# Two groups of squares ordered behind a later routing step in a fused attention and mixture-of-experts kernel

## Chip, core and metric

The kernel runs on one core of one Trainium2 chip. The metric is device microseconds of one execution; the time of the kernel before is the median of three runs, 1178.45 us (1178.34 to 1178.51).

## What is computed

Attention over channels, then a mixture of experts on its output. B = 4 batches, N = 5056 tokens, C = 256 channels, 8 experts, hidden width 1024.

```python
qn = q / (norm(q, axis=1) + 1e-06);  kn = k / (norm(k, axis=1) + 1e-06)
s = kn.transpose(0, 2, 1) @ qn / tau          # 256 x 256 for each batch
a = softmax(s, axis=-1)                        # with + 1e-09 on the sum
x = (v @ a).reshape(B * N, C)                  # 20224 tokens
logits = x @ w_gate + modality_bias[modality_id]
e = argmax(logits, axis=1); gate = softmax(logits)[e]
for each expert: out[mask] = gate * (relu(x[mask] @ w1[e]) @ w2[e])
```

The norms run over the tokens, so before the softmax of a batch the kernel needs two sums over all its tokens: the products k'q (256 x 256) and the sums of the squares of q and of k.

## The kernel before, in words

**Steps.** A batch is cut into 10 steps of 512 tokens (the last has 448); step g = 10 b + s is step s of batch b. For each step two kinds of work exist. `kq_pieces(b, s)` loads q and k, adds k'q to the bank `g` in TensorE (L368), squares q and k on ScalarE (L347, four instructions) and adds the squares to `acc` on VectorE (L349, four instructions). `va_pieces(b, s)` reads v, turns it, multiplies it with the attention weights (`xp`, L588), copies the rows (`x`), adds the logits (`L`, L601) and routes the tokens: `route` chooses the expert, `place` numbers the rows (`rp` on TensorE, L646 and L647, then `pi` on VectorE, L660), and `send` scatters the rows into a table in memory, `xs`, sorted by expert (four DMA issues of GpSimd for each step, L477).

**Turning v.** Steps 0 to 5 turn v on TensorE (`vtp`, L570). From step 6 on a DMA transpose of the SP queue brings it as `T` (L537), four DMAs gather its halves as `pl` (L514), and a copy on ScalarE (L521, the high halves, which the last two of the four bring) and one on VectorE (L522) join them as `vt`.

**Blocks.** A slot is one block of 512 rows of one expert. `pick` (L700 to L730) chooses the expert on VectorE once a step has been routed, and writes `pki`; the SP queue reads it and asks for the weights (`w1r` L791, `w2r` L795) and the rows (`Tx`, a DMA transpose of `xs`, L769). Slot 0 is picked after step 2 (START = 2), slot 1 after step 3. `tr_x` joins `Tx` to `xt` (L521, L522), and ScalarE and VectorE split it into `xh` and `xl` (L833, L834). Then come the matmuls `hp` (L848) and `y` (L869). From the first block on, TensorE has block after block, with routing and k'q of later steps between.

**Order.** The program is written piece by piece with `_interleave`, and a scheduler of the framework, with durations of its own, sets from that the order of the instructions on each engine. Each engine then runs its list strictly in that order and waits on semaphores. `order(ins, others)` (L463) binds an instruction behind others of its own engine in that list; it adds no wait. `routed[g]` holds the instructions which end the routing of step g: on VectorE `pi` and a reciprocal, on ScalarE the copy of the token numbers (L662), and later the choice of the slot (L728).

**Squares deferred.** For batch 1 the squares of some steps are not written where q and k are multiplied. `split` appends them to a list (`later`, L330), the list stands in `squares` under a number, and the end of loop round g runs the list of g + 1 (L1073). When it does, `act` and `dve` (L280 to L284) bind each square and each sum behind what `behind()` returns. The lists of batch 1's steps 1 and 2 are those that the change touches; those of steps 3 and later come from `product` (L980).

**Buffers that matter.** q and k of batch 1's steps 0, 1, 4, 5 share two buffers in turn: step 5's load must wait until the squares of step 1 have been read. q and k of steps 2 and 3 stand in buffers of `w1r` and `w2r`. The squares have three buffers for q and three for k. `xp` has three PSUM banks; a bank is free when ScalarE has copied the rows and VectorE has taken the logits.

Of the kernel before, what the change touches and what calls it, by code (L numbers as in the profile page):

```python
# [20 lines left out]
def _interleave(*streams):  # L21

    lists = [list(s) for s in streams if len(s) > 0]
    total = [len(x) for x in lists]
    at = [0] * len(lists)
    while any(a < n for a, n in zip(at, total)):
        i = min(
            (i for i in range(len(lists)) if at[i] < total[i]),
            key=lambda i: ((at[i] + 0.5) / total[i], i),
        )  # L30
        lists[i][at[i]]()
        at[i] += 1
# [3 lines left out]
def kernel(  # L36
# [40 lines left out]
    START = 2  # L77
# [103 lines left out]
    def pad_rows():  # L181

        ins = nc.sync.dma_start(
            xs[E * CAP : E * CAP + BLK, :].rearrange("(p t) c -> p t c", t=BLK // P),
            pad[0].bitcast(I32).unsqueeze(1).to_broadcast([P, BLK // P, XW]),
        )
        pads.append(ins.ins)
        tc.declare_no_dep(
            ins.ins, group="xr", reason="no expert has rows there"
        )  # L190
# [66 lines left out]
    def setup_bias(b, behind=()):  # L257
        shape = [P, NS * TT, E]
        bs = bsel[b] = p2.tile(shape, F32, tag="bsel", name=f"bsel_{b}")
        tmp = p1.tile(shape, F32, tag="btmp", name=f"btmp_{b}")  # L260
        for t, is_it, i in ((bs, ALU.is_ge, 1), (tmp, ALU.is_lt, 0)):
            ins = nc.vector.scalar_tensor_tensor(
                t, m1[:, b].rearrange("p s t -> p (s t)").unsqueeze(2).to_broadcast(shape), 0.5,
                small["mb"][:, i : i + 1, :].to_broadcast(shape), is_it, ALU.mult,
            )
            order(ins.ins, [i for n, i in behind if n == "dve"])
        nc.vector.tensor_tensor(bs, bs, tmp, ALU.add)
# [206 lines left out]
    routed = {}  # L474
# [20 lines left out]
    def slots_by(g):  # L495

        return max(0, g + 1 - START - sum(x <= g for x in SKIP))

    def lag(g):

        n = LAG
        for x in SKIP:
            n -= g >= x + n
        return n
# [424 lines left out]
    def run(pieces):  # L929
        for f in pieces:  # L930
            f()
# [19 lines left out]
    def once(blk, what):  # L951
        key = (blk["slot"], what)
        if key not in done:
            done.add(key)
            run(blk[what])

    def block_stream(blk, nxt):

        once(blk, "load")
        once(blk, "prep")  # L960
        body = list(blk["body"])
        if nxt is not None:
            once(nxt, "load")
            done.add((nxt["slot"], "prep"))
            split0, turn, split1 = nxt["prep"]
            for o, f in reversed(list(zip((7, 10, 13), (split0, lambda: turn(blk["evicted"][NJ - 3]), split1)))):
                body.insert(o, f)
        before = open_blk[0]["last"] if open_blk[0] is not None else []
        for i, f in enumerate(open_blk[0]["stores"] if before else []):
            blk["beside"].setdefault(2 + i, []).append(f)  # L970
        open_blk[0] = blk
        if not before:
            return [blk["first"]] + body
        return [blk["first"], before[0], body[0]] + before[1:] + body[1:]
# [17 lines left out]
    def ask(n):  # L992
        if n < len(tasks) and n not in loaded:
            loaded.add(n)
            product(n)[0]()

    def products_of(g):

        out = []
        for n, (at, b, i) in enumerate(tasks):  # L1000
            if at == g:
                out += [lambda n=n: ask(n)] if g <= first_block else []
                out += product(n)[1:]
                if g >= first_block and (b, i) != (1, NS - 1):
                    out.append(lambda n=n: ask(n + (1 if g == first_block else 2)))
        if g == first_block + 1:
            out.append(lambda: ask(min(n for n in range(len(tasks)) if tasks[n][0] > g) + 1))
        return out
# [1 line left out]
    va = [va_pieces(*divmod(g, NS)) for g in range(G)]  # L1010
    va[0][2]()
    run(va[0][0])
    squares = {1: [], 2: []}
    for s in BEFORE:
        if s == 0:
            run(kq_pieces(1, s))
        else:
            run(kq_pieces(1, s, lambda: routed[0], squares[s]))
    pad_rows()
    for g in range(G):  # L1020
        b, s = divmod(g, NS)
        streams = []
        for gg, blk in waiting:
            if gg <= g + 1 - lag(g + 1):
                once(blk, "load")
        if len(waiting) > 0 and waiting[0][0] <= g - lag(g):
            _, blk = waiting.pop(0)
            streams.append(block_stream(blk, waiting[0][1] if waiting and waiting[0][0] <= g + 1 - lag(g + 1) else None))
        soft = list(softmax_pieces(b)) if s == 0 and b > 0 else []
        begun = []  # L1030
        if g + 1 == first_block:
            split0, turned, split1 = waiting[0][1]["prep"]
            done.add((0, "prep"))
            begun = [split0, split1]
        own = list(va[g][1])
        if g - 1 in HELD:
            t = HELD[g - 1]
            own.insert(t + 1, lambda: va[g - 1][4]([copied[g, t]]))
        turn = []
        if g + 1 < first_block:  # L1040
            turn.append(va[g + 1][2])
        turn += va[g + 1][0] if g + 1 < G else []
        if g + 1 == first_block:
            turn.append(va[g + 2][2])
        if g == first_block:
            turn.append(va[g + 2][2])
        if first_block <= g + 2 < G:
            turn.append(va[g + 2][3])
        if g + 3 == first_block or first_block + 2 < g + 3 < G:
            turn.append(va[g + 3][2])  # L1050
        if g < first_block:
            streams.append(soft + turn + begun + own)
        else:
            streams.append(soft + own[:2] + turn[:1] + own[2:5] + turn[1:] + own[5:])
        if b + 1 < B:
            if b == 0 and s == 1:
                streams.append(list(kq_pieces(1, 2, lambda: routed[1], squares[2])))
            else:
                streams.append(products_of(g))
        _interleave(*streams)  # L1060
        if waiting and waiting[0][0] <= g + 1 - lag(g + 1):
            blk = waiting[0][1]
            once(blk, "load")
            if blk["slot"] == 0:
                turned(blk["evicted"][-1])
            once(blk, "prep")
        if s == NS // 2 + 2 and b < B - 1:
            setup_bias(b + 1, routed[g])
        n = slots_by(g)
        while chosen < n:  # L1070
            waiting.append((g, block_pieces(g, chosen, pick(g, chosen, False), False)))
            chosen += 1
        run(squares.get(g + 1, []))  # L1073
        if g == NS - 1:
            ask(min(n for n in range(len(tasks)) if tasks[n][0] > g) + 1)
# [84 lines left out]
```

## Time and profile before

| what | value |
|---|---|
| median of the runs | 1178.45 us |
| profiled execution, its own time | 1175.55 us |
| span from first to last instruction in it | 1173.7 us |
| PE busy | 1153.6 us (98%) |
| VectorE busy | 920.8 us (78%) |
| ScalarE busy | 806.1 us (69%) |
| GpSimd busy | 384.7 us (33%) |
| first matmul of a block (`hp`, slot 0) | 98.62 us |
| PE idle from 93.04 to 98.62 us, as one stretch before `hp` | 5.58 us |
| PE idle for k'q between 154 and 162 us | 1.8 us |

Times inside the program count from the first instruction of the span. PE is TensorE, DVE is VectorE, ACT is ScalarE, POOL is GpSimd, SP is the queue from which nearly all DMAs are issued; a row of an issuing queue has a q behind the engine. Names carry no buffer numbers in the profile, so the step or slot of a row follows from its place in the order. A k'q product of an unsplit step is one matmul in the program and two in the profile, since its operands are full float32.

### The profile page before, as it was taken

The numbers are of one execution on the slowest core, as the hardware profiler recorded it, in microseconds if no ns is written. First come the engines' busy times: TensorE is split into PE (matmuls) and PEld (weight loads), VectorE is DVE, ScalarE is ACT, GpSimd is POOL, SyncE is SP. The second block draws the span as 40 slices with busy tenths as digits, with TensorE's granted clock in tenths as the row PEclk, the third lists the DMA queues.
The fourth block names the chain that finished last, engine by engine and source line by source line (L and its number), as shares of the span: only waits on it lengthen the run. The fifth ranks groups of instructions, "written<-read, shape, count | busy, mean of one in ns | idle before, by whom it ended". The sixth has DMA issues, their size and how long they took to land.

```text
span 1173.7 us, 23358 instructions
## 1 busy us (share of the span) xinstructions
PE 1153.6 (98%) x7708; PEld 1054.6 (90%) x7708; DVE 920.8 (78%) x2591; ACT 806.1 (69%) x1655; POOL 384.7 (33%) x345
## 2 busy tenths in 40 slices
PE   8998999999999999999999999999999999999997
PEld 7896989999999999999999999999999999999997
DVE  6787989898888888888888888878777776686552
ACT  6676867877777777687777677767656666556553
POOL 0053333323333332333333333333333333344122
PEclk9998999999999999999999999999999999999999
DMA  8979999688777677759777776765876665464421
GB/s 293 307 236 230 269 239 255 173 248 217 199 200 201 196 192 206 208 159 234 204 209 203 210 202 162 167 182 158 207 218 172 187 176 158 134 178 136 136 86 35
DMA packets 285843, 228.38 MB, mean 195 GB/s; under 512 B 185064, under 2 KB 243944, under 8 KB 285712
## 3 DMA queue, kind: packets, MB, share of 16 engines
q1 hardware_dynamic: 270032, 185.19, 60.3%
q0 software_dynamic: 15680, 41.61, 10.4%
q8 instruction: 62, 1.02, 0.4%
q14 instruction: 69, 0.57, 0.2%
HBM read 128.79 MB, written 43.43 MB: 147 GB/s over the span
## 4 chain that ended last, share of the span: by engine, by line
PE 84%; issue 6%; DMA 5%; POOL 2%; DVE 2%; ACT 1%; SPq 0%; POOLq 0%; DVEq 0%; ACTq 0%
PE y L869 34%; PE hp L848 33%; PE xp L588 9%; PE g L368 6%; DMA k<-in_k_dram 2%; POOL out_dram L477 2%; DMA q<-in_q_dram 1%; DMA Tx<-xs 1%; DMA xs<-x,pi 0%; DMA pl<-T 0%; PE vtp L570 0%; PE gw L437 0%; ACT xt L521 0%; SPq L305 0%; PE atp L431 0%
## 5 line engine op out<-in xcount | busy, mean ns | idle before, releaser
L869 PE MATMUL y<-w2h,hh 128*128 128x256 f32 x1256 | 354.5, 282 | 0.0
L869 PE MATMUL y<-w2l,hh 128*128 128x256 f32 x1256 | 351.2, 280 | 0.0
L869 PE MATMUL y<-w2h,hl 128*128 128x256 f32 x1256 | 349.4, 278 | 0.1
L477 POOL DMA_INDIRECT xs<-x,pi x160 | 196.7, 1229 | 364.0 <-DVE pr L711 183.4
L477 POOL DMA_INDIRECT out_dram<-yo,gt x158 | 174.2, 1103 | 392.1 <-ACT hh L851 297.6
L848 PE MATMUL hp<-xh,w1h 128*128 128x512 f32 (+1 forms) x640 | 250.7, 392 | 5.6 <-ACT xh L833 5.6
L848 PE MATMUL hp<-xl,w1h 128*128 128x512 f32 (+1 forms) x640 | 250.7, 392 | 0.0
L848 PE MATMUL hp<-xh,w1l 128*128 128x512 f32 (+1 forms) x640 | 249.5, 390 | 0.0
L852 DVE SCALAR_TENSOR_TENSOR hl<-hp,hh 128x512 fp32r<-128x512 f32 (+1 forms) x320 | 216.7, 677 | 36.3 <-ACT hh L851 34.6
L869 PEld LDWEIGHTS y<-w2h,hh 128*128 128x128 f32 x1256 | 236.4, 188 | 9.3
L869 PEld LDWEIGHTS y<-w2l,hh 128*128 128x128 f32 x1256 | 236.4, 188 | 8.5
L851 ACT ACTIVATE hh<-hp 128x512 fp32r<-128x512 f32 (+1 forms) x320 | 188.7, 590 | 69.2 <-PE hp L848 69.0
L869 PEld LDWEIGHTS y<-w2h,hl 128*128 128x128 f32 x1256 | 235.3, 187 | 0.4 <-DVE hl L852 0.3
L814 ACT CAST w1h<-w1r 128x512 fp32r<-128x512 f32 x160 | 99.4, 621 | 166.4 <-PE hp L848 165.6
L821 DVE TENSOR_TENSOR w1l<-w1r,w1h 128x512 fp32r<-128x512 f32 x160 | 109.8, 686 | 91.1 <-ACT w1h L814 90.4
L848 PEld LDWEIGHTS hp<-xh,w1l 128*128 128x128 f32 x640 | 120.6, 188 | 26.0
L848 PEld LDWEIGHTS hp<-xh,w1h 128*128 128x128 f32 x640 | 120.4, 188 | 19.5 <-ACT xh L833 5.8
L848 PEld LDWEIGHTS hp<-xl,w1h 128*128 128x128 f32 x640 | 120.8, 189 | 13.4
L821 DVE TENSOR_TENSOR w2l<-w2r,w2h 128x512 fp32r<-128x512 f32 x160 | 109.8, 686 | 12.6 <-ACT w2h L814 11.3
L814 ACT CAST w2h<-w2r 128x512 fp32r<-128x512 f32 x160 | 100.8, 630 | 21.7 <-PE y L869 20.1
L588 PE MATMUL xp<-ah,vh 128*128 128x264 f32 x320 | 92.7, 291 | 0.1
L600 DVE COPY x<-xp 128x256 uint16<-128x256 uint16 x136 | 56.9, 419 | 45.5 <-ACT x L599 45.1
(161 smaller groups left out, 1817.1 us busy)
## 6 DMA issues: line engine op xcount, KB each, us to landing
w1r<-in_moe_w_dram SPq DMA_DIRECT2D x80, 512.0 KB, 4.7
w2r<-in_moe_w_dram SPq DMA_DIRECT2D x80, 512.0 KB, 4.6
q<-in_q_dram SPq DMA_DIRECT2D x35, 512.0 KB, 9.4
k<-in_k_dram SPq DMA_DIRECT2D x35, 512.0 KB, 5.5
pl<-T SPq DMA_DIRECT2D x120, 128.0 KB, 4.6
v<-in_v_dram SPq DMA_DIRECT2D x6, 512.0 KB
xs<-x,pi POOLq DMA_INDIRECT x160, 4.8
out_dram<-yo,gt POOLq DMA_INDIRECT x158, 3.2
```

Source lines behind the costliest of these rows:

```text
L368: nc.tensor.matmul(gram[b][:, m, :], x, y, start=first and m == 0 and i == 0, stop=last and i == len(seq) - 1, skip_group_check=True,)
L477: ins = nc.gpsimd.indirect_dma_start(out=dst, out_offset=bass.IndirectOffsetOnAxis(ap=idx, axis=0), in_=rows, in_offset=None, bounds_check ...
L588: nc.tensor.matmul(xp[:, 0:DE], a[:, h, t * P : (t + 1) * P], w[:, h, :], start=i == 0, stop=i == len(seq) - 1,)
L600: copied[g, t] = nc.vector.tensor_copy(planes[:, 0, :], halfwords[:, 0, :]).ins
L814: ins = nc.scalar.copy(hi, src).ins
L821: evicted[-1] = [ins, nc.vector.tensor_tensor(lo, src, hi.bitcast(F32), ALU.subtract).ins]
L848: nc.tensor.matmul(hp[:, 0:rows], w[:, h, fs], x[:, h, 0:rows], start=i == 0, stop=i == len(seq) - 1)
L851: relu = nc.scalar.activation(hh[:, 0:rows], hp[:, 0:rows], AF.Relu).ins
L852: low = nc.vector.scalar_tensor_tensor(hl[:, 0:rows], hp[:, 0:rows], 0.0, hh[:, 0:rows].bitcast(F32), ALU.max, ALU.subtract).ins
L869: ins = nc.tensor.matmul(y, a[:, tsl], w[:, j % 2, :], start=(j == 0 and i == 0 and t % per == 0), stop=(j == NJ - 1 and i == 2), skip_gro ...
```

## The change

The squares and sums of batch 1's steps 1 and 2 were run at the end of loop rounds 0 and 1, behind the routing of steps 0 and 1. Both lists now stand under the number 3, are run at the end of round 2, and are bound behind the routing of step 2 and the choice of slot 0. Nothing is added or left out: the same 8 squares on ScalarE and 8 sums on VectorE run, on the same data.

```diff
-    squares = {1: [], 2: []}
+    squares = {START + 1: []}
     for s in BEFORE:
         if s == 0:
             run(kq_pieces(1, s))
         else:
-            run(kq_pieces(1, s, lambda: routed[0], squares[s]))
+            run(kq_pieces(1, s, lambda: routed[START], squares[START + 1]))
...
             if b == 0 and s == 1:
-                streams.append(list(kq_pieces(1, 2, lambda: routed[1], squares[2])))
+                streams.append(list(kq_pieces(1, 2, lambda: routed[START], squares[START + 1])))
             else:
                 streams.append(products_of(g))
```

The scheduler then orders all engines anew between step 0 and about slot 4. Three places matter here. In the rows the first number behind a name is the step (for `xp`, `L`, `rp`, `pi`, `vt`, `pl`, `T`), the batch and step (for `q`, `k`, `sq`), or the slot (for `Tx`, `xt`, `xh`, `hp`, `w1r`); the last number only counts tiles.

TensorE, what stands around the row-number matmuls `rp` of step 2. Before:

```order
L588 MATMUL xp_3_3_915<-ah_0_440,vh_3_749 128x264
L588 MATMUL xp_3_3_915<-al_0_441,vh_3_749 128x264
L646 LDWEIGHTS trim_93
L646 MATMUL rp_2_819<-chosen_of_98,trim_93 128x40
L588 MATMUL xp_3_3_915<-ah_0_440,vl_3_750 128x264
L647 LDWEIGHTS onesb_86
L647 MATMUL rp_2_819<-run_2_814,onesb_86 128x40
```

Now:

```order
L588 MATMUL xp_3_0_884<-ah_0_440,vl_3_726 128x264
L368 MATMUL g_1_487<-q_1_3_860,k_1_3_862 128x256 x2
L646 LDWEIGHTS trim_93
L646 MATMUL rp_2_795<-chosen_of_98,trim_93 128x40
L368 MATMUL g_1_487<-q_1_3_860,k_1_3_862 128x256
L647 LDWEIGHTS onesb_86
L647 MATMUL rp_2_795<-run_2_790,onesb_86 128x40
```

Before, all eight k'q products of batch 1's step 3 and nearly all `xp` of step 3 stood ahead of `rp` of step 2; now two of the products and the first of the four `xp` do.

VectorE, behind the choice of slot 0 (`pki_0`), now:

```order
L726 CAST pki_0_830<-pk_0_828 1x2
L349 TENSOR_TENSOR acc_1_488<-acc_1_488,sq_1_1_0_q_834 128x2x256
L730 TENSOR_TENSOR nxt9_121<-nxt9_121,pr_0_820 128x9
L349 TENSOR_TENSOR acc_1_488<-acc_1_488,sq_1_1_0_k_837 128x2x256
L349 TENSOR_TENSOR acc_1_488<-acc_1_488,sq_1_1_1_q_840 128x2x256
L349 TENSOR_TENSOR acc_1_488<-acc_1_488,sq_1_1_1_k_843 128x2x256
L349 TENSOR_TENSOR acc_1_488<-acc_1_488,sq_1_2_0_q_846 128x2x256
L349 TENSOR_TENSOR acc_1_488<-acc_1_488,sq_1_2_0_k_849 128x2x256
L349 TENSOR_TENSOR acc_1_488<-acc_1_488,sq_1_2_1_q_852 128x2x256
L349 TENSOR_TENSOR acc_1_488<-acc_1_488,sq_1_2_1_k_855 128x2x256
L575 TENSOR_TENSOR vl_4_865<-vtp_4_1_875,vh_4_864 128x512
L601 TENSOR_TENSOR L_3_728<-xp_3_0_884,bsel_0_458 128x8
```

Before, four of these sums stood behind `pi` of step 0 and four behind `pi` of step 1; now all eight stand in one block ahead of the second half of step 4's v and of step 3's logits.

ScalarE, where the rows of slot 0 are turned (- before, + now):

```order
 L521 COPY xt_0_0_1270<-Tx_0_1133 128x512
 L521 COPY xt_0_1_1275<-Tx_0_1133 128x512
+L521 COPY vt_7_0_1394<-pl_7_1157 128x512
 L595 COPY x_5_991<-xp_5_3_1206 128x512
+L662 COPY x_5_991<-tokid_100 128x4
 L833 CAST xh_0_1268<-xt_0_0_1270 128x512
-L662 COPY x_5_991<-tokid_100 128x4
 L833 CAST xh_0_1268<-xt_0_1_1275 128x512
```

The first copy of step 7's v, `vt_7_0`, stood behind the third `hh` of slot 0 before; now it stands ahead of `xh` of slot 0. On the SP queue the order is the same up to the first use of `T_8`: `Tx_0`, the second weights of slot 0, the transpose `T_7`, the first `w1r` of slot 1, and the four `pl_7`. Behind `T_8` the row loads `Tx_2` and `Tx_3` now stand ahead of, instead of behind, the loads of q and k of step 6 and of the weights of slot 2.

## Prediction

> **What bounds the kernel now.** I read the page's busy times first, then the waits of PE in the first 250 us, then windows, chain and rows around the first block.
>
> ```profile
> PE 1153.6 (98%) x7708; PEld 1054.6 (90%) x7708; DVE 920.8 (78%) x2591; ACT 806.1 (69%) x1655; POOL 384.7 (33%) x345
> ```
>
> ```profile
> PE hp L848 <- ACT xh L833: 5.6, 1, 5.6
> PE g L368 <- DVE qs L324: 1.6, 2, 1.1
> ...
> PE g L368 <- DVE ks L324: 0.2, 1, 0.2
> ```
>
> PE is busy in 98% of the span. The columns of the waits are total us, times, longest: behind the start-up, PE stands still for 5.6 us once, ahead of the first block, and for 1.8 us (1.6 + 0.2) in k'q between 155 and 161 us. Every other delay is hidden behind PE's own work. So a change between these places moves the end only if it moves the first `hp`, closes the 1.8 us, or makes a new stop.
>
> The chain of waits (start, length) and the last rows ahead of `hp`:
>
> ```profile
> 82.39 5.62 DMA xs<-x,pi
> ...
> 88.72 7.49 DMA Tx<-xs
> 96.23 0.50 ACT xt L521
> ...
> 98.05 0.53 ACT xh L833
> ```
>
> ```profile
> 98.62 1.22 PE L848 MATMUL hp<-xh,w1h 128*128 128x512 f32 x2 [5.58 <-ACT xh L833]
> ```
>
> The first block starts when step 2's last scatter has landed (88.01), `Tx_0` has been asked for (88.72) and landed (96.21), and ScalarE has made `xt` and `xh`. PE stops from 93.04 (98.62 - 5.58) to 98.62. The stop also costs clock; in the windows (edges, length, busy time and instructions of PE, PEld, DVE, ACT, POOL, then PE's granted clock):
>
> ```profile
> 94.00:96.00 2.00, 0.00 (x0) 0.00 (x0) 0.00 (x0) 0.00 (x0) 0.00 (x0) 1.00 1.06 309
> 96.00:98.00 2.00, 0.00 (x0) 0.00 (x0) 0.91 (x4) 1.77 (x4) 0.00 (x0) 0.77 1.78 285
> 98.00:99.00 1.00, 0.38 (x1) 0.38 (x2) 0.79 (x4) 1.00 (x4) 0.68 (x1) 0.50 0.08 23
> ...
> 103.00:104.00 1.00, 1.00 (x5) 0.48 (x3) 0.00 (x0) 0.90 (x2) 0.60 (x1) 0.55 1.05 401
> 104.00:105.00 1.00, 1.00 (x7) 0.80 (x8) 0.60 (x6) 0.47 (x2) 0.00 (x0) 1.00 1.01 359
> ```
>
> A mean of 0.77 in 96 to 98 puts the fall to 0.50 at 97.1, 4.0 us into the stop; 0.55 in 103 to 104 puts the return at 103.9. PE thus works at half clock for 5.3 us (98.6 to 103.9), a loss of 2.65 us beside the 5.58.
>
> **The change, part by part.**
>
> *Sums and squares leave routing 0 and 1.* They are 8 of each:
>
> ```profile
> 60.98 0.68 DVE L349 TENSOR_TENSOR acc<-acc,sq_q 128x512 f32<-128x512 f32 x1
> 61.58 0.68 DVE L349 TENSOR_TENSOR acc<-acc,sq_k 128x512 f32<-128x512 f32 x1
> ```
>
> One sum starts 0.60 us behind the other: 8 x 0.60 = 4.8 us of VectorE, of which PE saw nothing. The squares run on ScalarE, which is less loaded; moving them costs nothing while ScalarE is ahead of VectorE there, and 8 squares at some 0.6 us would be another 4.8 us if it were not.
>
> *Step 2's row numbers come earlier.* On TensorE six of eight k'q products and 17 of 24 `xp` no longer stand ahead of `rp`.
>
> ```profile
> 68.66 3.62 PE L368 MATMUL g<-q,k 128*128 128x256 f32 x16
> ...
> 74.14 0.28 PE L588 MATMUL xp<-ah,vh 128*128 128x264 f32 x1
> 74.26 0.28 PE L588 MATMUL xp<-al,vh 128*128 128x264 f32 x1
> ```
>
> Eight products (16 in the profile) took 3.62 us, six take 2.7; `xp` start 0.12 apart, 17 take 2.1. Together 4.8 us earlier for `rp` and `pi` of step 2.
>
> ```profile
> 73.98 0.98 POOL L477 DMA_INDIRECT xs<-x,pi  x1 [0.30 <-issue]
> 78.54 0.98 POOL L477 DMA_INDIRECT xs<-x,pi  x1 [3.58 <-ACT x L662]
> ```
>
> GpSimd stood idle for 3.58 us ahead of step 2's scatter (78.54); its last issue of step 1 (73.98) moves earlier as well, since step 1 is spared its own four sums. So the 4.8 us pass through the four issues and the landing, and `Tx_0` is asked for at 83.9 instead of 88.72. Its rows land at 83.9 + 7.5 = 91.4. Were that all, `xh` would be ready 2.4 us later, at 93.8, and the stop would be nearly closed.
>
> *`vt_7_0` stands in the way.* The order of ScalarE now has `vt_7_0`, `x_5`, and the token copy ahead of `xh` of slot 0. An engine runs its list in order, so the first block now waits for `pl_7`, which the SP queue asks for behind `Tx_0`, the weights and `T_7`:
>
> ```profile
> 88.72 2.43 SPq L769 DMA_TRANSPOSE Tx<-xs  x1
> ...
> 93.08 5.84 SPq L537 DMA_TRANSPOSE T<-in_v_dram  x1
> 99.81 0.39 SPq L791 DMA_DIRECT2D w1r<-in_moe_w_dram  x1
> 101.05 2.65 SPq L514 DMA_DIRECT2D pl<-T  x4
> ```
>
> ```profile
> DMA to landing us min/median/max: 4.5/5.1/5.8
> ```
>
> Before, `T_7` was asked for 4.4 us behind `Tx_0`, the first `pl_7` 12.3 behind it, and the last of the four (0.68 apart, 2.65 in all) 14.4 behind it. This piece of SP's list is unchanged and moves as a whole, so the last `pl_7` is asked for at 83.9 + 14.4 = 98.3 and lands, by the median of the second view, at 103.4. `pki_1`, which stands in that list, is no obstacle: VectorE made the choice of slot 1 near 83 and will be some 5 us later, near 88, while SP comes to it at about 94. What ScalarE then still has to do:
>
> ```profile
> 97.48 0.57 ACT L595 COPY x<-xp 128x512 uint16<-128x512 uint16 x1
> 97.94 0.62 ACT L833 CAST xh<-xt 128x512 fp32r<-128x512 f32 x1
> 98.46 0.20 ACT L662 COPY x<-tokid 128x4 int32<-128x4 int32 x1
> 98.56 0.62 ACT L833 CAST xh<-xt 128x512 fp32r<-128x512 f32 x1
> ...
> 108.07 0.76 ACT L521 COPY vt<-pl 128x512 uint16<-128x512 uint16 x1
> 108.70 0.62 ACT L347 ACTIVATE sq_q<-q 128x512 f32<-128x512 f32 x1
> ```
>
> By the distances of their starts `vt` takes 0.63, `x` 0.46, the token copy 0.10, and from `xh` to `hp` it was 98.62 - 97.94 = 0.68. So `hp` starts at 103.4 + 1.9 = 105.3 instead of 98.62: **+6.7 us**. With the landing at 4.5 or 5.8 it is +6.1 or +7.4.
>
> *Where the 4.8 us of sums go.* They stand as a block on VectorE ahead of step 4's `vl` and step 3's logits. The routing of step 4 ended on VectorE at 91.4 and will at about 96:
>
> ```profile
> 91.37 0.16 DVE L705 TENSOR_TENSOR pr<-end,nxt 128x9 f32<-128x9 f32 x1
> ```
>
> `rp` of step 4 and some 18 `xp` behind it (2.2 us) stand ahead of `hp` on PE, so PE comes to `hp` at 97 to 98.5. The stop that begins there covers the block; without that stop it would cost 4 to 5 us against the 93.04 at which PE now comes. The same work stands ahead of `hp` on PE before and now, so nothing else changes sides.
>
> *The clock.* The new stop is 7 to 8 us long, longer than the 4.0 after which the clock fell. `hp` again starts at half clock and pays the same 2.65: net 0. Bounds: 0 to +0.5, if a cold clock lasts a little longer this time.
>
> *The 1.8 us at 155 to 161.* There VectorE waited for step 9's `pl`.
>
> ```profile
> 128.00 1.41 ACT L521 COPY vt<-pl 128x512 uint16<-128x512 uint16 x2 [2.13 <-DMA pl<-T]
> ...
> 149.19 0.78 ACT L521 COPY vt<-pl 128x512 uint16<-128x512 uint16 x1 [2.76 <-DMA pl<-T]
> ```
>
> ScalarE was held 2.76 us by it. PE's work shifts by 6.7 us, while SP's list does so only by part: `Tx_0` to `pl_7` are 4.8 us earlier, and `Tx_2`, `Tx_3` now stand ahead of the q and k loads. `pl_9` should thus come 2 us or more earlier against PE and close the gap. I take -1.8; bounds 0 and -1.8, since no more can be won where PE has no other gap.
>
> **Sum:** +6.7 + 0 - 1.8 = +4.9 us. The profiled execution would go from 1175.55 to 1180.5; the run median, 2.9 above that execution, to 1178.45 + 4.9 = **1183.4 us**.
>
> **The rivals.**
>
> *A: a shorter way to `pl_7`.* For step 6 the same two DMAs stood closer:
>
> ```profile
> 55.12 3.18 SPq L537 DMA_TRANSPOSE T<-in_v_dram  x1
> ...
> 60.73 1.30 SPq L514 DMA_DIRECT2D pl<-T  x2
> ```
>
> That is 5.6 us from `T` to `pl`, where step 7 took 8.0 beside the still running `Tx_0`. With 5.6, and a landing of 4.7, `hp` starts 2.8 us sooner, at 102.5: +3.9 - 1.8 = +2.1, 1180.5. Against it: `T_7` still follows `Tx_0` at the same distance. The stop would be 4.0 to 5.5 us, so the clock might just stay up (-2.65 more), but mostly not.
>
> The row for that is the fall 4.0 us into the stop, at 97.1. [...]
>
> *B: faster.* Were `pl_7` there by the time PE comes to `hp`, the first block would start at about 97.8, without the half clock: -0.8 - 2.65 - 1.8 = -5.2, 1173.2. That needs `pl_7` landed by 97.8 - 1.9 = 95.9, 12.0 us behind `Tx_0`'s start. The shortest rows give 4.4 + 5.6 + 2.0 (first to last `pl`) + 4.5 = 16.5. It decides itself at that one place, and no row comes near it.
>
> *C: longer.* `x_5` is held behind `vt_7_0` too, so step 5's routing and its scatter are late by 6 to 7 us. `Tx_2` waits for the scatter of step 4, whose token copy stands behind `x_5`, and it now stands ahead of the q and k loads of step 6 and of slot 2's weights. Then `pl_9` is no earlier, the 1.8 us stay, and about 2 us join them at 120 to 160 us: +6.7 + 2 = +8.7, 1187.2. For it:
>
> ```profile
> 105.79 3.13 SPq L769 DMA_TRANSPOSE Tx<-xs  x1
> ...
> 117.09 0.52 SPq L305 DMA_DIRECT2D q<-in_q_dram  x1
> 121.46 2.58 SPq L514 DMA_DIRECT2D pl<-T  x4
> ```
>
> SP is the queue on which all this hangs, and a held `Tx_2` holds the loads behind it. Against it: between 105.79 and 117.09 there are 11 us with few issues, and a block of PE's work lies ahead of each.
>
> *D: the change doesn't do what it says.* If ScalarE's squares or the token copy hold step 2's scatter where it was, `Tx_0` stays at 88.72 and `pl_7` lands at 108.2: `hp` at 110.1, +11.5 - 1.8 = +9.7, 1188.2. In the order the squares stand behind the routing, so this is unlikely.
>
> **How the numbers follow.** Main 0.64, A 0.13, B 0.05, C 0.15, D 0.03. The main case's own range is 1181.4 to 1186.0: a landing of 4.5 to 5.8 us (-0.6 to +0.7), SP's piece up to 1 us shorter because step 2's rows meet less traffic, and 0 to 1.8 us of recovery. The 8-in-10 range adds A below and most of C above: 1180.0 to 1187.0. A measurement of this kernel tells 0.2% (2.4 us) from no change, so "same" is 1176.1 to 1180.8. It holds two thirds of A and a sliver of the main case, 0.11; faster is B and A without the half clock, 0.06; slower is the rest, 0.83.
>
> **What would show it.** The scatter of step 2 should start near 73.7 and `Tx_0` near 83.9; if not, D. ScalarE should idle for some 10 us ahead of one `vt`, released by the DMA `pl`, and then run `vt`, `x`, token copy, `xh` in a row, with `hp` at 104.5 to 106; a `hp` near 102.5 is A. PE's longest wait should be 7 to 8 us, with the clock at 0.50 for about 5 us behind it. The k'q waits near 160 should be gone; if they stay or grow, C. The forecast is wrong if `hp` starts at or before 98.6, or if PE has a new stop of over 1 us after 106.

## The result

The changed kernel took 1187.20 us (median of 6 runs, 1185.72 to 1188.44) beside 1178.48 us for the kernel before in the same series (a series is a set of runs of both kernels made side by side): a ratio of 1.0079, with a 95% interval of 1.0064 to 1.0093. It is slower, as forecast, by 8.7 us where 4.9 were forecast, and 0.2 us past the end of the range.

The profiled execution has a span of 1186.7 us, 13.0 more than the profiled one before. That one was 2.9 us under its median and this one, with 1188.44 us, 1.2 over, so the traces lie further apart than the 8.7 us of the medians. Its waits of PE in the first 250 us (total, times, longest) and the last rows ahead of the first block:

```profile
PE hp L848 <- ACT x L662: 7.2, 1, 7.2
PE rp L646 <- DVE chosen_of L622: 5.7, 2, 3.1
...
PE g L368 <- DVE qs L324: 1.5, 2, 1.0
```

```profile
111.21 1.22 PE L848 MATMUL hp<-xh,w1h 128*128 128x512 f32 x2 [7.20 <-ACT x L662]
```

The chain of waits of that trace, from `T_7` to the first block:

```profile
93.57 10.44 DMA T<-in_v_dram
...
106.14 2.98 DMA pl<-T
...
109.22 0.76 ACT vt L521
109.97 0.45 ACT x L595
```

The mechanism is the forecast one: `T_7`, `pl_7`, `vt_7_0`, `x`, and only then the first block. ScalarE stood idle for 9.32 us ahead of that `vt`. But `hp` is at 111.21, not at 105.3; against 98.62 before it is 12.6 us late, and these 12.6 are nearly all of the 13.0 by which the spans of the two traces differ. The k'q waits near 160 (1.5 + 0.2 us) are still there.

Why 111 and not 105? Step 2's scatter, in the rows of GpSimd:

```profile
78.64 0.97 POOL L477 DMA_INDIRECT xs<-x,pi  x1 [6.96 <-ACT vh L574]
79.92 4.92 POOL L477 DMA_INDIRECT xs<-x,pi  x1 [0.30 <-issue]
```

It begins at 78.64, as before the change (78.54), though its `rp` stands 4.8 us of matmuls earlier in TensorE's list. The row copies of step 2 on ScalarE and the matmuls that they follow show why:

```profile
65.83 0.28 PE L588 MATMUL xp<-ah,vl 128*128 128x264 f32 x1
...
66.56 0.28 PE L588 MATMUL xp<-ah,vl 128*128 128x264 f32 x1
```

```profile
67.49 0.58 ACT L595 COPY x<-xp 128x512 uint16<-128x512 uint16 x1 [1.42 <-PE xp L588]
70.41 0.58 ACT L595 COPY x<-xp 128x512 uint16<-128x512 uint16 x1 [2.34 <-PE vtp L570]
73.26 1.07 ACT L595 COPY x<-xp 128x512 uint16<-128x512 uint16 x2 [2.26 <-PE xp L588]
```

The two matmuls end the first and the second `xp` tile of step 2, at 66.11 and 66.84. By the program the copies wait for nothing but these, and ScalarE is idle, yet they start 1.4 and 3.6 us later, and the third at 73.26, 5.7 us behind its matmul. With three banks for `xp`, TensorE then stops twice ahead of an `xp` (0.74 us at 68.33, 1.02 at 71.25), by the program for a bank, and the logits and `rp` come late (PE's 3.1 us for `chosen_of`): `rp` begins at 76.23, where it began at 76.42 before the change. The next section shows that this is not so in every series.

### The profile page after: what moved, and what is told of

Read it like the earlier page. It is cut to its first block, busy times and chain, and to the rows that moved or that the text cites. A ratio compares the mean times of both kernels' runs of the same rounds, so it can differ in the third digit from the quotient of the medians.

```text
span 1186.7 us, 23369 instructions
## 1 busy us (share of the span) xinstructions
PE 1156.0 (97%) x7708; PEld 1056.4 (89%) x7708; DVE 921.6 (78%) x2591; ACT 807.0 (68%) x1655; POOL 390.0 (33%) x345
## 3 DMA queue, kind: packets, MB, share of 16 engines
q0 software_dynamic: 15680, 41.61, 10.2%
q8 instruction: 62, 1.02, 0.4%
## 4 chain that ended last, share of the span: by engine, by line
PE 82%; issue 7%; DVE 4%; DMA 3%; ACT 2%; POOL 2%; SPq 0%; POOLq 0%; DVEq 0%; ACTq 0%
PE y L869 32%; PE hp L848 31%; PE g L368 9%; PE xp L588 9%; POOL out_dram L477 2%; DMA pl<-T 2%; DMA T<-in_v_dram 1%; DVE hl L852 1%; SPq L514 0%; DVE vl L575 0%; ACT x L595 0%; DVE w2l L821 0%; PE gw L437 0%; DMA k<-in_k_dram 0%; DVE acc L349 0%
## 5 line engine op out<-in xcount | busy, mean ns | idle before, releaser
L477 POOL DMA_INDIRECT xs<-x,pi x160 | 202.2, 1264 | 369.7 <-DVE pr L711 183.5
```

Source lines behind the costliest of these rows:

```text
L477: ins = nc.gpsimd.indirect_dma_start(out=dst, out_offset=bass.IndirectOffsetOnAxis(ap=idx, axis=0), in_=rows, in_offset=None, bounds_check ...
```

## The experiments

**The changed kernel again, and the kernel before again.** No edit.

> The changed kernel, unaltered, for a second trace of it. In the first trace step 2's scatter began at 78.64 us, not at 73.7, because the row copies x of step 2 began 1.4 to 5.7 us after their last xp matmul, and T_7 took 10.6 us to its first pl where step 7 took 8.0 before. If these belong to the order, they are there again: scatter within 0.5 us of 78.6, hp of slot 0 within 1.5 us of 111.2. If they belong to the one execution, the scatter begins at 73.5 to 75 and hp starts at 105 to 107. The time is the same by both, 1186 to 1188 us.

> The kernel before, unaltered, for a second trace. The first came from an execution of 1175.55 us, 2.9 below the median. If the difference lies in the first block, hp starts about 2.9 us later than 98.62, at 101 to 102; if it lies elsewhere, hp stays at 98.6 within 0.5 us and another stretch of PE idle time is longer by 2 to 3 us.

In this series the changed kernel took 1181.02 us beside 1176.09, a ratio of 1.0041 (1.0025 to 1.0056), +4.9 us. The second trace of the changed kernel, GpSimd, then ScalarE and TensorE:

```profile
73.18 0.98 POOL L477 DMA_INDIRECT xs<-x,pi  x1 [1.60 <-ACT vh L574]
74.46 4.90 POOL L477 DMA_INDIRECT xs<-x,pi  x1 [0.31 <-issue]
...
80.95 0.98 POOL L477 DMA_INDIRECT xs<-x,pi  x1 [0.30 <-issue]
```

```profile
66.05 2.77 ACT L595 COPY x<-xp 128x512 uint16<-128x512 uint16 x4
...
104.08 0.76 ACT L521 COPY vt<-pl 128x512 uint16<-128x512 uint16 x1 [10.74 <-DMA pl<-T]
104.72 0.57 ACT L595 COPY x<-xp 128x512 uint16<-128x512 uint16 x1
105.32 0.20 ACT L662 COPY x<-tokid 128x4 int32<-128x4 int32 x1
105.42 1.13 ACT L833 CAST xh<-xt 128x512 fp32r<-128x512 f32 x2
```

```profile
106.08 1.22 PE L848 MATMUL hp<-xh,w1h 128*128 128x512 f32 x2 [8.63 <-ACT xh L833]
```

Here the four copies are in time (66.05 and following), the scatter begins at 73.18 (forecast: 73.7), `pl_7` has landed at 104.08 (103.4), and `hp` is at 106.08 (105.3). So the order alone does not make the copies late. Nor is it a matter of single executions: all six runs of the first series lie between 1185.72 and 1188.44, all nine of this one between 1178.93 and 1182.78, where the expectation had 1186 to 1188 either way. It goes by series. The kernel before has `hp` at 97.93 in its second trace, 0.7 earlier than in the first. With 1173.47 us this was another short execution, so it does not tell where the 2.9 us between the first trace and its median lie. Of the 2.1 us between the two traces, 0.7 lie in `hp` and 1.2 in the half clock behind it (last section).

**`vt_7_0` behind the third `hh`.** All of the change stays, with one more tie in ScalarE's order:

```diff
-                    [cast[g - 1]] if g == first_block else (),
+                    [cast[g - 1]] if g == first_block else held7() if g == first_block + 1 and h == 0 else (),
...
```

`held7()` returns the latest `hh` of slot 0.

> The changed kernel with one more tie in ScalarE's order: vt_7_0 stands behind the third hh of slot 0, where it stood before the change. Everything else of the change stays. Theory 1, the first block waits for pl_7 through vt_7_0: ScalarE's wait of 9.3 us ahead of xh goes, hp starts 1.5 to 3 us after xt, at 97 to 102 us instead of 111.2, and the time falls by 9 to 12 us, to 1175 to 1179 us. Theory 2, the loss is made upstream (late copies of step 2, late Tx_0) and vt_7_0 only fills a wait that is there anyway: the time falls by less than 3 us, to 1184 to 1187.

1178.51 us, a ratio of 1.0024 (1.0010 to 1.0037) to the kernel before: 2.5 us less than the changed kernel beside it. `hp` starts at 98.27 without a stop. Neither theory had the size right: the stop moved.

```profile
PE y L876 <- ACT yo L890: 5.0, 1, 5.0
```

```profile
130.91 1.38 ACT L526 COPY vt<-pl 128x512 uint16<-128x512 uint16 x2 [8.01 <-DMA pl<-T]
```

TensorE, now some 8 us ahead, meets the same trap one step later: ScalarE is held for 8.01 us by `vt_8`, and slot 0's output copies `yo` stand behind it. The granted clock was then at half from 132.3 to 139.1 us, of which TensorE works 6.0 us; that is another 3.0 us lost, by estimate.

**`pl_8` ahead of slot 2's rows.** The same kernel, and `Tx_2` tied behind `pl_8` on SP:

```diff
...
                 if slot == 1:
                     turning.append(ins.ins)
+                if slot == 2:
+                    order(ins.ins, halved.get(first_block + 2, []))   # the four pl_8
```

> The kernel with vt_7_0 behind the third hh, and with one more tie on SP: the rows of slot 2 (Tx_2) behind pl_8, as before the change. With vt_7_0 behind the third hh alone the stop at hp was gone, but a stop of 5.0 us stood at 129 us, where y waited for yo, which ScalarE held 8.0 us behind step 8's vt. Theory 1, the change hurts where ScalarE's order and SP's order disagree, and pl_8 is late because Tx_2 stands ahead of it: pl_8 is asked for 2 to 4 us earlier, the stop at 129 falls below 2.5 us, and the time falls by 2.5 to 5 us, to 1173 to 1176 where the kernel before has 1176. Theory 2, pl_8 is late by T_8, whose place does not change: the stop stays at 4 to 6 us and the time within 1.5 us of 1178.5.

The stop fell to 1.9 us, as the first theory had it, and `pl_8` was asked for 1.4 us earlier; but the time was 1180.43 us, 5.3 above the kernel before (1.0048, 1.0028 to 1.0068). A new stop took its place:

```profile
PE hp L861 <- DVE hl L865: 4.0, 1, 4.0
PE rp L655 <- DVE chosen_of L631: 2.6, 1, 2.6
PE y L882 <- ACT yo L896: 1.9, 1, 1.9
```

The forecast of a gain was wrong. The trace shows the same trap a third time, now for step 9: VectorE stands idle for 5.77 us and ScalarE for 6.47 ahead of their `vt` copies at 152.19 and 152.93, for `pl_9`, which SP asks for at 145.47. The next `hh` (154.08) and `hl` (154.81) stand behind these copies, and `hp` goes on at 155.55.

**`T_7` ahead of `Tx_0`.** ScalarE's order stays that of the change, `vt_7_0` ahead of `xh`; only SP's list differs:

```diff
         def load_x():
+            if slot == 0:
+                va[first_block + 1][2]()      # T_7; Tx_0 is tied behind it
...
-        if g + 1 == first_block:
-            turn.append(va[g + 2][2])
```

> The changed kernel with ScalarE's order as it is (vt_7_0 ahead of slot 0's xh), but with the transpose T_7 asked for on SP ahead of Tx_0 and no longer behind slot 0's second weights. Theory 1, the first block waits for pl_7: T_7 starts at 76 to 78, pl_7 lands before 96, the wait of 10.7 us ahead of vt_7_0 shrinks below 3 us, and hp starts at 96 to 100 instead of 106; the time falls as much as with vt_7_0 moved, by 2 to 6 us. Theory 2, the place of vt_7_0 is what costs, whatever its data: hp stays at 104 to 107 and the time within 1.5 us of the changed kernel.

> The changed kernel with T_7 ahead of Tx_0, a second time, as control beside the run above: its matmuls and row copies up to step 2 are those of the changed kernel, so late copies are seen here too. In a series without late copies: again within 1 us of the kernel before. In one with them: Tx_0 near 89 instead of 85, pl_7 landed by then, hp at 101 to 104 instead of 109 to 111, and 2 to 5 us above the kernel before instead of 8.7 to 9.9.

1174.96 us beside 1175.10 for the kernel before (0.9997, 0.9986 to 1.0008), and in another series 1.0009 (0.9995 to 1.0022): the whole loss of the change is gone.

```profile
76.20 4.87 SPq L538 DMA_TRANSPOSE T<-in_v_dram  x1
85.42 2.01 SPq L773 DMA_TRANSPOSE Tx<-xs  x1
```

```profile
98.44 0.76 ACT L522 COPY vt<-pl 128x512 uint16<-128x512 uint16 x1 [4.68 <-DMA pl<-T]
...
99.77 1.14 ACT L839 CAST xh<-xt 128x512 fp32r<-128x512 f32 x2
```

```profile
100.44 0.74 PE L854 MATMUL hp<-xh,w1h 128*128 128x512 f32 x2 [2.79 <-ACT xh L839]
```

`T_7` is asked for at 76.20 in place of 88.86, `vt_7_0` starts at 98.44 in place of 104.08, and `hp` 5.6 us earlier, still behind `pl_7`: the wait of 4.68 us is longer than the 3 expected, and `hp` at 100.44 just outside its 96 to 100. So it is the lateness of `pl_7`, through `vt_7_0`, that costs, and not the place of the copy as such. The second run fell in a series without late copies, so what this edit does to those is not known.

**Step 1's or step 2's squares alone.**

```diff
-    squares = {START + 1: []}
+    squares = {2: [], START + 1: []}        # step 2's stay behind step 1's routing
...
-                streams.append(list(kq_pieces(1, 2, lambda: routed[START], squares[START + 1])))
+                streams.append(list(kq_pieces(1, 2, lambda: routed[1], squares[2])))
```

> Only step 1's four squares and sums go behind step 2's routing; those of step 2 stay behind step 1's as before. In this order vt_7_0 stands behind slot 0's first matmuls again. Theory 1: no long wait of ScalarE ahead of xh, so no loss: 1176 to 1180 us, hp at 96 to 100. Theory 2, any move of sums behind step 2's routing costs by the block on VectorE that holds up step 3's logits: about half of the loss, 1181 to 1184.

```diff
-    squares = {START + 1: []}
+    squares = {1: [], START + 1: []}        # step 1's stay behind step 0's routing
...
-            run(kq_pieces(1, s, lambda: routed[START], squares[START + 1]))
+            run(kq_pieces(1, s, lambda: routed[0], squares[s]))
```

> Only step 2's four squares and sums go behind step 2's routing; those of step 1 stay behind step 0's. In this order vt_7_0 stands behind slot 0's xh but ahead of its first hh. Theory 1: hp itself starts at 94 to 100, ScalarE then waits 3 to 6 us for pl_7 and PE stops for as much behind the second hp; the time lies 0 to 3 us above the kernel before. Theory 2 (each moved group of sums costs its share): 2 to 3 us above the kernel before, with the stop ahead of hp.

Step 1's alone: 1175.93 us, 0.9996 (0.9980 to 1.0011), no difference in time, as the first theory had it, though `hp` starts at 94.62, earlier than its 96 to 100, and a stop of 2.6 us behind `pl_7` follows at 107.85. Step 2's alone: 1179.77 us, 1.0041 (1.0025 to 1.0057), 4.7 above the kernel before, more than either theory had. It shows the trap on another engine. VectorE, then TensorE:

```profile
91.65 0.18 DVE L607 TENSOR_REDUCE mx<-L 128x4 f32<-128x32 f32 x1
102.50 0.46 DVE L522 COPY vt<-pl 128x512 uint16<-128x512 uint16 x1 [10.67 <-DMA pl<-T]
```

```profile
103.83 0.80 PE L848 MATMUL hp<-xl,w1h 128*128 128x512 f32 x1 [10.40 <-DVE xl L834]
```

In this order VectorE's half of `vt_7_0` stands ahead of `xl` of slot 0. The first two `hp` matmuls run at 91.97; then TensorE stands for 10.40 us until `pl_7` has landed.

**The two cures put together.** Three kernels with `T_7` ahead of `Tx_0`: on step 1's squares alone, on the kernel before, and on step 2's squares alone with both halves of `vt_7_0` behind slot 0's third `hh` and `hl` as well.

> Step 1's squares moved alone, with the transpose T_7 ahead of Tx_0 on SP. Alone the first edit gave the time of the kernel before, with two stops of PE: 2.0 us at 90.4 for step 3's logits and 2.6 us at 105.3, where hl waited behind ScalarE's wait for pl_7. If that second stop is pl_7's, it goes, with the half clock behind it (1.7 to 3.4 us at half rate): 2 to 4 us below the kernel before. If Tx_0 is held up by T_7 as much as pl_7 gains, the stop moves to the first hp and the time stays within 1 us of the kernel before.

> The kernel before with T_7 ahead of Tx_0 on SP, as a control: there the first block waits for Tx_0 (step 2's scatter), not for pl_7. Theory 1 (a stop goes only when its own last wait is shortened): hp stays at 97 to 100 and the time within 1 us of the kernel before, or up to 2 us above it if T_7 holds the queue when Tx_0 could start. If an earlier T_7 helps by itself, by the later steps' transposes: 3 us or more below.

> Step 2's squares moved alone, T_7 ahead of Tx_0, and step 7's first join behind the third hh and hl on ScalarE and VectorE. With the first edit alone PE stopped for 10.4 us behind two matmuls of hp, since VectorE waited 10.7 us for pl_7 with the vt copy that stood ahead of xl; 4.7 us above the kernel before. Theory 1: with that copy behind, xl is there at once, the stop falls below 2 us, and the time falls by 5 to 9 us, to 0 to 4 us below the kernel before. Theory 2, PE's lead is lost at the next wait (y behind yo near 129, or hp behind hl near 150, as it was with vt_7_0 behind the third hh): within 2 us of the kernel before.

None beats the kernel before. Step 1's with the early `T_7` took 1177.07 us (1.0021, 1.0009 to 1.0032), slower: `T_7` now holds `Tx_0` (asked for at 91.39, not 86.84), and stops of 1.1 and 2.8 us stand ahead of and inside the first `hp`. The kernel before with the early `T_7`: 1.0006 (0.9993 to 1.0019), a time as the first theory expected where `Tx_0` and not `pl_7` comes last; `T_7` holds `Tx_0` there too, until 92.40, and `hp` is at 100.09. So an early `T_7` gains nothing by itself. Step 2's with both: 1.0007 (0.9997 to 1.0018), so the 4.7 us of its edit are gone; the stop of 10.4 fell only to 5.4, and now waits for `Tx_0`.

**How often the copies are late.** The changed kernel in four more series, with the kernel before beside it, and a variant in which step 1's scatter waits for step 2's second row copy, so that eight scatter issues no longer follow each other without a pause:

```diff
-    HELD = {3: 3, 4: 3}
+    HELD = {1: 1, 3: 3, 4: 3}
```

> The changed kernel once more. In one trace of it the row copies of step 2 began up to 5.7 us late and slot 0's hp at 111.2, in the other they were in time and hp began at 106.1; the medians stood 8.7 and 4.9 us above the kernel before. If the late copies are an accident of single executions, the median is again 4 to 6 us above the kernel before and hp starts at 105 to 107. If they are a matter of the chip or of the way in which it runs that day, the result falls near one of the two again, with hp and median going together: 106 and +5, or 111 and +9.

> The changed kernel a fourth time, beside the other three of this call. Two of three series had it 4.9 us above the kernel before (hp at 105 to 106), one 8.7 us (hp at 111.2, row copies of step 2 late by up to 5.7 us). If the late copies were an accident of that one series, this is again +4 to +6 us with hp at 105 to 107; if they come back, +8 to +9 with hp at 110 to 112.

> The changed kernel a fifth time. Three later series had it 4.3 to 4.9 us above the kernel before, with step 2's scatter at 73.2 to 73.7 and hp at 104 to 106; only the first had 8.7 us, with the scatter at 78.6 and hp at 111.2. If the late scatter is a state that comes back, one of the next two series falls at +8 to +9 with the scatter near 78.6; if it was an accident, both are at +4 to +6.

> The kernel before again, for its trace. Its first block waits for Tx_0 alone; if the kernel before has a state of late copies too, step 2's scatter stands 3 to 5 us behind 78.5. Else it is at 78 to 79, hp at 97.5 to 99.

> The changed kernel as control for the run beside it. By now five series: +4.3 to +4.9 us with the row copies of step 2 in time (three), +8.7 and +9.9 with copies up to 5.7 us late (two). It falls into one of the two groups, with the trace's scatter of step 2 at 73.2 to 73.7 or at 78.4 to 78.6.

> The changed kernel, with step 1's scatter waiting for the second row copy of step 2, so that eight scatter issues no longer run without a pause from 61 to 72 us (before the change there was a pause of 2.7 us between step 0's and step 1's). If the late copies come from the dense scatters and this series has them in the control, the copies are in time here: scatter of step 2 at 73 to 76 and 3 to 5 us less than the control. If the dense scatters have no part in it, copies and time are within 1 us of the control. In a series without late copies it is within 1.5 us of the control by both, and tells nothing of their cause.

> Step 1's scatter waiting for step 2's second row copy, a second time, since the first series had no late copies and told nothing of their cause. In a series with late copies (the run beside it shows them): dense scatters as the cause give copies in time, scatter of step 2 at 73 to 76 and +4 to +6 us against the kernel before; no part in it gives the scatter at 78 or later and +8 to +10. In a series without them: +4 to +6 us.

The third, fourth and sixth series gave ratios of 1.0046 (1.0028 to 1.0064), 1.0040 (1.0026 to 1.0054) and 1.0047 (1.0030 to 1.0063), +4.3 to +5.1 us, with `hp` at 105.27, 104.01 and 105.35. The fifth gave 1185.51 us beside 1175.61, 1.0083 (1.0066 to 1.0100), +9.9 us. Its trace again has the late scatter:

```profile
78.36 0.98 POOL L477 DMA_INDIRECT xs<-x,pi  x1 [6.35 <-ACT sq_k L347]
```

```profile
108.66 1.22 PE L848 MATMUL hp<-xh,w1h 128*128 128x512 f32 x2 [4.87 <-ACT x L662]
```

So it is a condition that comes back, in two of six series, and time, scatter and `hp` go together in it. The kernel before, traced in the fifth series, has its scatter at 78.12 and its copies of step 2 at 68.55, where the squares let them start. A late copy is seen there all the same, a little further on:

```profile
83.06 0.59 ACT L595 COPY x<-xp 128x512 uint16<-128x512 uint16 x1 [1.12 <-issue]
```

The last matmul of its tile ends at 81.48, and the profile shows nothing else that it waits for; in the first trace the same copy starts 0.27 us behind its matmul (81.91 and 82.18), without a gap. So the condition is not one of the new order alone. In the kernel before it costs nothing that shows: `hp` is at 96.63, ahead of the expected 97.5 to 99, and the median of that series, 1175.61, is like those of the others. The traces taken in these two series (the changed kernel's in both, the kernel before's in the fifth) hold some 15,300 records of semaphore updates, where all other traces hold some 18,450. The fifth series is the only one known to have run on chip 0; the others ran on chips 14, 14, 5 and 10, and for the first no chip is on record. Chip, day and series are thus not told apart. The variant with the pause took 1.0046 (1.0029 to 1.0063) and 1.0039 (1.0014 to 1.0063), but both of its series had no late copies, so it tells nothing of their cause. The cause of the late copies is open.

## Why the prediction was right and wrong

**The bound and the mechanism: right in the main.** `hp` waits for `vt_7_0`, and making `pl_7` earlier removes the whole loss without touching ScalarE's order. Moving `vt_7_0` removes the stop too, though TensorE then loses most of that lead at 129 us (5.0 us and the half clock behind it). But the end does not move with the first `hp` alone: with the early `T_7` it is at 100.44, 1.8 us later than in the first trace of the kernel before, at the same time in all, and with step 1's squares alone 4.0 earlier, again at the same time. So other stops of TensorE and their half clock count beside it.

**Step 2's row numbers 4.8 us earlier: right in four series, wrong in two, among them the one that was forecast.** Here failed the step "Together 4.8 us earlier for `rp` and `pi` of step 2", and with it the 4.8 us that were to pass through the four issues. It counted TensorE's matmuls and took for granted that ScalarE's copies follow them. In the first series they did not: `rp` came 0.2 us earlier, the scatter began at 78.64, and `Tx_0` was asked for 5.6 us behind its forecast. These are nearly all of the 5.9 us by which `hp` missed its own. Why the copies were late is open. This is rival D's outcome, with `Tx_0` at 89.47 and `hp` at 111.21 where D gave 88.7 and 110.1, for another reason than D named. The squares that were taken out of this stretch had covered such a delay before: ScalarE was busy with them until 68.5. That last point is argued from the order, not shown by a run.

**Where the sums go: right.** TensorE stops for 2.6 us ahead of `rp` of step 4 (92.59 in the second trace), but comes to `hp` at 97.45 (forecast: 97 to 98.5), and the wait for `pl_7` covers it.

**From the scatter to `Tx_0`: right in sum, by two errors that cancel.** The forecast had 3.85 us from the first to the last of the four issues and 6.3 to `Tx_0`. In the second trace the last issue is at 80.95, 7.8 us behind the first, and `Tx_0` at 83.76 only 2.8 behind it. The issue of 4.90 us among them is told below.

**From `Tx_0` to `vt_7_0`: right in sum, again by two errors.** The first `pl_7` came 15.3 us behind `Tx_0` (99.01 - 83.76) where 12.3 were taken, since `T_7` was asked for 5.1 us behind `Tx_0` instead of 4.4 and its first `pl_7` 10.2 us behind it instead of 8.0. The landing behind the last issue took 3.0 us instead of 5.1. Rival A's shorter way did not come about.

**ScalarE's last 1.9 us: right.** From `vt_7_0` to `hp` 2.00 us in all traces of the changed kernel.

**The clock: 0 in the middle, but the bounds too narrow.** In the second traces TensorE works at half clock for 5.0 us from `hp` on after the change and for 2.9 before, a loss that is 1.0 us larger; in the first traces it is 3.0 and 5.3, 1.1 us smaller. Forecast was 0 to +0.5.

**The 1.8 us at k'q: mis-sized.** They were to close. In the first trace 1.7 us remain of 1.8, in the second 1.3 of 1.3, in the fourth and fifth series 1.0 each, in the sixth 0.3, and in the third they are gone. So the term held in one or two of six traces. Rival C's figure, 1187.2, is the measured time, but by chance, for its mechanism is not there: no stop of over 0.4 us stands between 112 and 160 in the first trace. Only the fourth series shows a little of it, 1.5 us for `y` behind `yo`.

**The range**, as a distance from the kernel before (+1.6 to +8.6 us), held four of six series. At the top it had no room for D's outcome, whose chance was put at 0.03. That the four series lie at +4.3 to +5.1, where the sum gave +4.9, is in part luck: between the second traces `hp` moved by 8.2 us instead of 6.7, the k'q waits did not close, and the spans differ by 9.4. These two executions lie 1.8 above and 2.6 below the medians of their series; what sets them apart is not shown. The kernel before took 1175.0 to 1176.1 in the five later series and 1178.5 in the first; beside those the first series would lie some 11 to 12 us above it.

## What to carry to other kernels

When work is moved off an engine's list, look first at what the scheduler then puts in its place: here a copy that waits for a DMA came to stand ahead of the work that all else waits for, on ScalarE in one order and on VectorE in another. Making the transfer earlier cured such a wait here without touching the order, as long as it did not hold up the transfer that came last; moving the copy handed most of the lead to the next wait of the same kind. And work that is "hidden" may itself cover another delay, which is argued here and not shown: before taking it away, ask what the engine would be waiting for without it.

## What had not been expected of the hardware

**A GpSimd issue took 4.9 us instead of 1.0 beside VectorE's eight sums.** It is the second issue of step 2's scatter, and it does so in all traces of the changed kernel (4.90 to 4.92 us). VectorE of the second trace:

```profile
73.54 0.67 DVE L349 TENSOR_TENSOR acc<-acc,sq_q 128x512 f32<-128x512 f32 x1
...
77.83 0.67 DVE L349 TENSOR_TENSOR acc<-acc,sq_k 128x512 f32<-128x512 f32 x1
78.43 0.67 DVE L575 TENSOR_TENSOR vl<-vtp,vh 128x512 fp32r<-128x512 f32 x1
```

The last sum ends at 78.50; the issue that began at 74.46 ends at 79.36, 0.86 us behind it, a little less than a usual issue (0.98). With the four sums of step 1 alone the same issue takes 2.50 us:

```profile
77.86 2.50 POOL L477 DMA_INDIRECT xs<-x,pi  x1 [0.30 <-issue]
```

In the second trace the `vl` behind the last sum ran from 78.43 to 79.10, beside the end of the issue. But not every issue beside such sums takes that long. In the first trace of the kernel before, sums run back to back from 68.97 to 71.47 and from 83.17 to 85.64, and these issues pass beside them:

```profile
69.85 1.27 POOL L477 DMA_INDIRECT xs<-x,pi  x1 [2.71 <-DVE acc L349]
...
84.19 1.11 POOL L477 DMA_INDIRECT xs<-x,pi  x1 [0.75 <-ACT x L595]
```

What decides between the two is open, and no run shows what holds the issue. From these rows, 1.27 and 1.11 us where 0.98 is usual, the prediction could have named a risk, for the block was put beside the scatter; a price of 4.9 us could not be read from them.

**The half clock lasted 3.4, 6.8 and 10.2 us.** In the second trace of the kernel before (the columns are those of the windows above):

```profile
97.00:98.00 1.00, 0.07 (x1) 0.07 (x1) 0.48 (x4) 1.00 (x4) 0.37 (x1) 0.70 1.39 262
98.00:99.00 1.00, 1.00 (x3) 0.81 (x4) 1.00 (x5) 0.76 (x2) 0.69 (x2) 0.50 1.09 241
...
100.00:101.00 1.00, 1.00 (x4) 0.80 (x3) 0.98 (x6) 0.00 (x0) 0.70 (x2) 0.60 0.88 111
```

and in that of the changed kernel:

```profile
100.00:101.00 1.00, 0.00 (x0) 0.00 (x0) 0.00 (x0) 0.00 (x0) 0.00 (x0) 0.90 0.39 138
...
111.00:112.00 1.00, 1.00 (x7) 0.77 (x7) 0.52 (x6) 1.00 (x2) 0.00 (x0) 0.98 1.01 335
```

The clock was at half from 97.4 to 100.8 in the one (3.4 us) and from 100.8 to 111.0 in the other (10.2 us); in the first trace of the kernel before it was 6.8 us (97.1 to 103.9). In the first trace of the changed kernel it lasted 3.4 us twice (76.7 to 80.1 and 100.6 to 104.0) and 6.8 us once (107.4 to 114.2). Why these lengths lie so near to multiples of 3.4 is not shown. The price of the stop ahead of `hp` differs between executions of the kernel before: 1.45 us behind a stop of 5.12 us (2.9 us at half clock behind `hp`), 2.65 behind one of 5.58, and nothing in the third trace, where the stop is 3.32 us and `hp` runs at full clock (0.72 us for the first two matmuls, which took 1.22 at half clock). Differences of this kind, 1.2 us between two nearly equal stops of one kernel, belong to no edit.
